# A fused chunk-attention and mixing kernel: x and u turned by DMA transposes, and a new order with the loads in it

## The chip, the cores and the metric

The kernel runs on one core of one Trainium2 chip. The metric is the device time of one execution in microseconds (us). A run is called slow when it is over 1.5% above the fastest run of the same kernel in the same set, and fast otherwise. Means and ratios below use fast runs alone; medians are over all runs. Engines: PE (matmuls), DVE and ACT (vector and scalar work), POOL (issues all loads), SP (SyncE, issues stores and, in the change, transposes).

## The reference

All inputs are float32 in memory; the kernel works in fp16. There are 8 batches, 8 heads, 576 positions, head size 64, model width 512.

```python
# attention in 9 chunks of 64, each for itself
scores = scale * q_c @ k_c.T ;  attn = softmax(scores) ;  x = attn @ v_c    # x: [8, 576, 512]
# mixing
theta = x @ w_theta
zr, zi = x * cos(theta), x * sin(theta)
y  = w_tok_r @ zr + w_tok_i @ zi          # over the 576 positions
u  = x + y
out = u + relu(u @ w_ch)
```

## The kernel before

Two batches make a pair (4 pairs, 1152 rows, 9 tiles of 128 rows); each pair has five groups of one or two tiles, 20 in all. The program is a list of items, searched offline, that fixes the order on every engine. `a1` transposes q and k on PE, `a2` does scores and exp, `a3` attention times V, giving x; `a4` transposes x on PE; `a5` does theta with cos and sin; `z` the products; `tw` transposes the token weights; `yh` and `y` mix over positions and add x, giving u transposed; `w` multiplies u by w_ch; `st` adds and stores. The first number of an item is the pair (in `y`, pair, batch of the pair, block of 128 channels; in `w` and `st`, pair and tile).

```python
ORDER = """
a1.0.0:0 a2.0.0:0 a1.0.1:3 a1.0.2:2 a3.0.0.0:0 a2.0.1:0 a3.0.0.1:0 a2.0.2:0 a3.0.2.0:0
a4.0.0:1 a4.0.2:3 a3.0.1.0:0 a3.0.1.1:0 a5.0.2:0 a4.0.1:1 a5.0.0:0 z.0.2.0:0 z.0.0.0:0
...                                                                      # cut
a2.0.4:0 yh.1.1:0 a3.0.4.0:0 a1.1.0:0 a4.0.3:0 w.0.0:0 a2.1.0:0 a3.0.4.1:0 st.0.0:0
...                                                                      # cut
""".split()

def a4(p, g, bits):                      # x of one group, turned on PE
    ...
    for jj in range(n):
        for db in range(NDB):            # 4 blocks of 128 channels
            nc.tensor.transpose(psv[:, db, jj * P : jj * P + P],
                                st[p]["x", g][:, jj, db * P : db * P + P], id16)
    copy(bits & 1, xT[:, :, x_col(j0) : x_col(j0) + n * P], psv)

def w(p, j):                             # u @ w_ch, and u itself turned back by the identity
    for db in range(NDB):
        nc.tensor.matmul(ps[:, 0:DM], uT[:, db, j * P : j * P + P], wch16[:, db, :], ...)
        nc.tensor.matmul(ps[:, DM + db * P : DM + db * P + P], uT[:, db, j * P : j * P + P], id16)
    nc.scalar.activation(out=r, in_=ps[:, 0:DM], func=AF.Relu)

def out_tile(p, j):
    nc.vector.tensor_tensor(out=o, in0=ps[:, DM : 2 * DM], in1=r, op=ALU.add)
    nc.sync.dma_start(out[...], o)

# loads: in a fixed sequence on POOL; group i is loaded once a1 of group i-7 stands in the program
```

The softmax here doesn't subtract the row's maximum and nothing guards it: scores larger than these inputs give would overflow.

## Time and profile before

| | before |
|---|---|
| time | 219.24 us median of 3 (218.29 to 221.8) |
| span of the profiled run | 217.4 us |
| PE work, by spacings | 190.1 us |
| PE end | 213.1 us, so 23.0 us of PE time lost and a tail of 4.3 us |

### The profile page before, as it was taken

To read this page: it belongs to the slowest core of one execution; us is meant where nothing else is said; L and a number is where in the kernel's file an instruction comes from. 1 tells how busy PE (TensorE), PEld (TensorE's weight loads), DVE (VectorE), ACT (ScalarE), POOL (GpSimd) and SP (SyncE) were. 2 spreads that over 40 slices of the span, in tenths; PEclk is the share of its full clock that TensorE was granted. 3 is DMA by queue.
4 is the path that set the end of the run, shared out by engine and by line. 5 is a ranking of instruction groups with operands and counts; after the bars stand their busy time and mean duration, and the time that the engine had idled before them with its cause. 6 is when DMAs were issued, how large, how long until landed. Compare 5 with 4: busy or idle time off the path is not lost.

```text
span 217.4 us, 6721 instructions
## 1 busy us (share of the span) xinstructions
PE 198.8 (91%) x2994; PEld 138.8 (64%) x2994; DVE 132.8 (61%) x230; ACT 118.5 (54%) x138; POOL 85.1 (39%) x118
## 2 busy tenths in 40 slices
PE   0485999989999999999997999999999999999992
PEld 0374568765677875667886664776766675777750
DVE  0148486747977575869776837567836655275273
ACT  2244484338968689838574468753085446321242
POOL 7896468679885698765920000000000000000000
PEclk9999999999999999999999999999999999999999
DMA  6999999999999999999990012112121313113136
GB/s 59 177 131 166 200 181 179 177 170 132 166 221 196 165 132 181 213 228 192 142 164 5 3 48 72 51 51 48 53 96 51 121 48 100 48 49 147 48 124 216
DMA packets 83612, 26.92 MB, mean 124 GB/s; under 512 B 76288, under 2 KB 78976, under 8 KB 83584
## 3 DMA queue, kind: packets, MB, share of 16 engines
q0 software_dynamic: 77696, 16.54, 86.0%
q1 hardware_dynamic: 5888, 9.96, 13.5%
q8 instruction: 23, 0.38, 0.7%
q14 instruction: 5, 0.04, 0.0%
HBM read 33.06 MB, written 9.44 MB: 195 GB/s over the span
## 4 chain that ended last, share of the span: by engine, by line
PE 80%; DMA 6%; DVE 4%; POOL 3%; issue 3%; ACT 2%; POOLq 0%
PE ps_y L455 28%; PE ps_theta L377 14%; PE ps_uw L475 13%; PE ps_qkT L266 6%; PE ps_y L434 4%; PE ps_sT L292 4%; DMA wtheta<-in_moe_w_theta_dram 3%; PE ps_uw L482 3%; PE ps_xT L348 3%; PE ps_x L320 3%; DMA qk<-in_k_dram 3%; POOL v L176 2%; PE ps_wT L218 1%; POOL qk L155 1%; DVE o L494 1%
## 5 line engine op out<-in xcount | busy, mean ns | idle before, releaser
L455 PE MATMUL ps_y<-wT,z 128*128 128x288 f16 x448 | 59.8, 286 | 1.2 <-issue 1.2
L455 PEld LDWEIGHTS <-z 128*128 128x128 f16 x448 | 42.2, 98 | 13.8 <-issue 1.5
L176 POOL DMA_DIRECT2D v<-in_v_dram x56 | 42.0, 766 | 17.3 <-DMA qk<-in_k_dram 10.7
L475 PE MATMUL ps_uw<-wch,uT 128*128 128x512 f16 x144 | 42.5, 380 | 0.0
L488 ACT ACTIVATE relu<-ps_uw 128x512 f32<-128x512 f32 x36 | 21.6, 600 | 37.6 <-PE ps_uw L482 37.2
L463 DVE TENSOR_TENSOR uT<-ps_y,xT 128x576 f16<-128x576 f32 x28 | 21.2, 755 | 28.8 <-PE ps_y L455 28.7
L494 DVE TENSOR_TENSOR o<-ps_uw,relu 128x512 f32<-128x512 f32 x36 | 24.5, 686 | 11.7 <-ACT relu L488 11.5
L482 PE MATMUL ps_uw<-id,uT 128*128 128x128 f16 x144 | 31.5, 219 | 0.0
L377 PE MATMUL ps_theta<-wtheta,xT 128*128 128x512 f16 x128 | 30.5, 384 | 0.1
L266 PE MATMUL ps_qkT<-id,qk 128*64 128x128 f16 (+1 forms) x640 | 22.5, 227 | 6.4 <-DMA qk<-in_q_dram 5.7
L387 ACT ACTIVATE cos<-ps_theta,pihalf 128x1024 f16<-128x1024 f32 (+1 forms) x20 | 20.6, 1029 | 12.7 <-PE ps_theta L377 12.4
L334 DVE TENSOR_TENSOR x<-ps_x,recip 128x512 f16<-128x512 f32 x36 | 24.9, 691 | 1.2
L266 PEld LDWEIGHTS <-qk 128*64 128x64 f16 (+1 forms) x640 | 19.1, 118 | 8.8 <-DMA qk<-in_q_dram 5.7
L299 ACT ACTIVATE eT<-ps_sT 128x1024 f16<-128x1024 f32 (+1 forms) x20 | 18.3, 940 | 11.4 <-PE ps_sT L292 11.4
L475 PEld LDWEIGHTS <-uT 128*128 128x128 f16 x144 | 14.1, 98 | 14.7
L197 DVE COPY kT<-ps_qkT 128x1024 f16<-128x1024 f16 (+1 forms) x13 | 15.2, 1169 | 12.5 <-ACT qT L199 12.5
L155 POOL DMA_DIRECT2D qk<-in_k_dram x24 | 19.1, 797 | 5.5 <-DMA qk<-in_q_dram 2.9
L377 PEld LDWEIGHTS <-xT 128*128 128x128 f16 x128 | 12.1, 99 | 13.6 <-issue 0.9
L155 POOL DMA_DIRECT2D qk<-in_q_dram x24 | 19.3, 805 | 2.1 <-POOLq L558 0.8
L391 ACT ACTIVATE sin<-ps_theta 128x1024 f16<-128x1024 f32 (+1 forms) x20 | 18.7, 933 | 0.0
L199 ACT COPY kT<-ps_qkT 128x1024 f16<-128x1024 f16 (+1 forms) x7 | 8.4, 1224 | 14.2 <-DVE qT L197 14.2
L292 PE MATMUL ps_sT<-qT,kT 64*64 64x64 f16 x576 | 12.3, 223 | 3.9 <-ACT kT L199 2.9
(51 smaller groups left out, 212.0 us busy)
## 6 DMA issues: line engine op xcount, KB each, us to landing
out_dram<-o SPq DMA_DIRECT2D x32, 256.0 KB, 2.1
qk<-in_q_dram POOLq DMA_DIRECT2D x16, 256.0 KB, 6.9
qk<-in_k_dram POOLq DMA_DIRECT2D x16, 256.0 KB, 8.2
v<-in_v_dram POOLq DMA_DIRECT2D x40, 64.0 KB, 6.4
v<-in_v_dram POOLq DMA_DIRECT2D x16, 128.0 KB, 6.3
out_dram<-o SPq DMA_DIRECT2D x8, 128.0 KB, 2.9
wnat<-in_moe_w_tok_r_dram POOLq DMA_DIRECT2D x2, 288.0 KB, 8.9
wnat<-in_moe_w_tok_i_dram POOLq DMA_DIRECT2D x2, 288.0 KB, 9.6
```

The lines of the kernel that those rows point to most:

```text
L155: nc.gpsimd.dma_start(t[(pp // 2) : (pp // 2) + m // 2, ti].rearrange("p h t d -> p h (t d)"), src.rearrange("h (p t) d -> p h (t d)", t=2),)
L176: nc.gpsimd.dma_start(v16[pp : pp + m, sl, :, 0:D], v[2 * p + bb, :, s0 : s0 + m, :].rearrange("h s d -> s h d"),)
L266: nc.tensor.transpose(psv[par * D : par * D + D, w, e, tk, 0:rows], t[0:rows, w, 2 * e + par, tk, :], id16[0:rows, 0:rows],)
L292: nc.tensor.matmul(psv[kh * CH : kh * CH + CH, par, i, e, :], kT[par * D : par * D + D, e, c0 : c0 + CH], qT[par * D : par * D + D, e, c0 ...
L334: nc.vector.tensor_tensor(out=xo, in0=px[:, :, :, 0:D], in1=recip.broadcast_to((P, 2, NE, D)), op=ALU.mult,)
L377: nc.tensor.matmul(ps[:, jj * DM : jj * DM + DM], xt[:, db, :], wtheta16[:, db, :], start=(db == 0), stop=(db == NDB - 1),)
L455: nc.tensor.matmul(psv[:, hf, 0:HS], zt[:, db * P : db * P + P], wT[:, kt, hf * HS : hf * HS + HS], start=(kt == 0), stop=(kt == 2 * KT),)
L463: nc.vector.tensor_tensor(out=uT_tile(p)[:, db, sl].rearrange("p (f c) -> p f c", f=2), in0=psv[:, :, 0:HS], in1=xT_tile(p)[:, db, sl].rea ...
L475: nc.tensor.matmul(ps[:, 0:DM], uT[:, db, j * P : j * P + P], wch16[:, db, :], start=(db == 0), stop=(db == NDB - 1),)
L482: nc.tensor.matmul(ps[:, DM + db * P : DM + db * P + P], uT[:, db, j * P : j * P + P], id16,)
L488: nc.scalar.activation(out=r, in_=ps[:, 0:DM], func=AF.Relu)
L494: nc.vector.tensor_tensor(out=o, in0=ps[:, DM : 2 * DM], in1=r, op=ALU.add)
```

## The change

Intent: take transposes off PE. x of 18 of the 20 groups and u of the last five batches go through DMA transposes on SyncE; relu and add of those u tiles become one DVE instruction; some stores move to POOL. The list of items was searched again, now with the loads (`lq`, `lv`, `lt`, `lw`, `lc`) as items in it. Bit 16 of an `a4` item selects the DMA; bit 2 of `st` selects POOL.

```diff
-a1.0.0:0 a2.0.0:0 a1.0.1:3 a1.0.2:2 a3.0.0.0:0 a2.0.1:0 a3.0.0.1:0 a2.0.2:0 a3.0.2.0:0
-a4.0.0:1 a4.0.2:3 a3.0.1.0:0 ...
+lw.0:0 lq.0.0:0 a1.0.0:3 lq.0.2:0 lq.0.1:0 a2.0.0:0 a1.0.2:2 lv.0.2:0 a1.0.1:3 a2.0.2:0
+lq.0.3:0 a2.0.1:0 a3.0.2.0:0 a1.0.3:0 lv.0.1:0 a3.0.1.0:0 lq.0.4:0 ...
 (the rest of the two lists is cut)
+    U_DMA = 3
+    def xt(p, g):
+        if n == 1:
+            nc.sync.dma_start_transpose(xm, x[:, 0, :])
+            return
+        for jj in range(n):
+            nc.sync.dma_start_transpose(xT[:, :, c0 : c0 + P], x[:, jj, :])
     def a4(p, g, bits):
+        if bits & 16:
+            xt(p, g)
+            ...
+            return
+    def ut(p, bb, db):
+        nc.sync.dma_start_transpose(un_tile(p, bb)[:, :, db * P : db * P + P], uT_tile(p)[:, db, cols])
     def w(p, j):
-            nc.tensor.matmul(ps[:, DM + db * P : ...], uT[:, db, j * P : j * P + P], id16)
+            if 2 * p + int(j >= KT) < U_DMA:       # only the first three batches
+                nc.tensor.matmul(ps[:, DM + db * P : ...], uT[:, db, j * P : j * P + P], id16)
     def out_tile(p, j, bits):
+            nc.vector.scalar_tensor_tensor(out=o, in0=ps[:, 0:DM], scalar=0.0, in1=un_tile(...)[...],
+                                           op0=ALU.max, op1=ALU.add)
-            nc.sync.dma_start(out[...], o)
+        eng = nc.gpsimd if bits & 2 else nc.sync
+            eng.dma_start(out[...], o)
 (the rule that placed the loads is gone; the cut parts are the same in kind)
```

## The prediction

> **What bounds the kernel now.** I read the page first (busy shares, slices, queues, chain), then the chain in order of time, then the timeline of POOL, which issues all loads. From the page:
>
> ```profile
> span 217.4 us, 6721 instructions
> PE 198.8 (91%) x2994; PEld 138.8 (64%) x2994; DVE 132.8 (61%) x230; ACT 118.5 (54%) x138; POOL 85.1 (39%) x118
> PE   0485999989999999999997999999999999999992
> DMA  6999999999999999999990012112121313113136
> q0 software_dynamic: 77696, 16.54, 86.0%
> PE 80%; DMA 6%; DVE 4%; POOL 3%; issue 3%; ACT 2%; POOLq 0%
> ```
>
> PE is busy almost everywhere after the first slices and carries 80% of the chain. But the DMA row stands at 9 from slice 2 to slice 21 (about 115 us) while the loads run, and then drops to 0 to 3. So there are two resources: PE for the whole span, and the load stream for the first half.
>
> PE's busy time counts latencies that overlap, so I use spacings. From the chain of waits in order of time (start, duration, what):
>
> ```profile
> 14.16 7.46 DMA wtheta<-in_moe_w_theta_dram
> 21.75 1.87 PE ps_theta L377 x4
> ...
> 74.58 1.01 PE ps_qkT L266 x32
> ...
> 161.05 2.21 PE ps_y L455 x18
> 163.25 1.73 PE ps_theta L377 x8
> ...
> 166.06 0.45 PE ps_xT L348 x8
> 166.51 0.22 PE ps_uw L475
> 166.78 0.22 PE ps_uw L475
> ```
>
> Eight PE transposes of x take 0.45 us, that is 56 ns each. A 512-column matmul takes 1.73/8 = 0.216 us. In the last stage (w), matmuls follow each other every 0.27 us (166.51, 166.78), so the identity matmul between two of them costs 0.27 - 0.216 = about 0.056 us. An output tile of w is 4 x 0.27 = 1.09 us.
>
> Summing the whole list of PE work with such spacings: y 28 x 2.25 = 63.0; y of the first batch in halves 9.2; w 36 x 1.09 = 39.2; theta 16 x 1.73 + 4 x 0.86 = 31.1; q/k transposes 16 x 1.01 + 4 x 0.62 = 18.6; scores 8.8; attention x V 9.2; x transposes 16 x 0.45 + 4 x 0.22 = 8.1; token weights 2.7. Total **190 us** of work.
>
> The last PE matmul starts at 212.9 us in the timeline and ACT's last relu, which waits for it, at 213.15, so PE lacks work for 23 us in all. After that come relu (0.60), the last add (0.69) and the last store: 217.4 - 213.15 = 4.3 us of tail.
>
> Where are the 23 us? Just before the first q/k transpose of pair 2, group 1 (started at 74.5) the list holds 53.8 us of work, so 20.7 us are already lost; only 2.3 us are lost later. The early loss is set by loads: the first theta waits for its weights until 21.75. POOL's timeline shows their pace:
>
> ```profile
> 1.24 1.02 POOL L155 DMA_DIRECT2D qk<-in_q_dram  x1 [0.79 <-POOLq L558]
> ...
> 41.29 0.69 POOL L176 DMA_DIRECT2D v<-in_v_dram  x1 [0.69 <-DMA wch<-in_moe_w_ch_dram]
> ...
> 89.67 0.90 POOL L155 DMA_DIRECT2D qk<-in_q_dram  x1
> ...
> 107.95 2.31 POOL L176 DMA_DIRECT2D v<-in_v_dram  x3
> ```
>
> 112 loads are issued from 1.24 to 107.95 + 2.31 = 110.26, one per **0.973 us**; the issue at 41.29 was held until an earlier load had landed, as are most gaps of POOL in the list of waits (10.7 us of waits on k loads alone). The DMA section gives about 6.5 us from issue to landing. Check: before the transpose at 74.5, 67 loads are in line, 1.24 + 67 x 0.973 + 6.5 = 72.9 us. So the present order is just in time for its loads there.
>
> **What the Trainium skill says.** (1) "Perfetto Trace Analysis", Identifying the Most-Contended Engine: matmul busy share does not measure headroom because matmuls are pipelined. The trace agrees: 198.8 us busy for 190 us of work, and each matmul's record (219 to 380 ns) is longer than its spacing. (2) "TensorE: Matmul & The Clock Gate", Step-by-step: what each phase is for: spacing 216 ns at 512 columns and 55.6 ns at 128. The trace gives 0.216 and 0.056 us. (3) "DMA: Bandwidth & Descriptors", Issuing engines are not separate DMA queues: all queues run on the same 16 DMA engines and interleave. So SyncE's transposes meet POOL's loads. How much this costs no trace here shows directly; POOL issued 16 loads from 63.96 to 79.79 (0.99 us each), nearly without stores beside them, and 15 from 79.79 to 95.63 (1.06 us each), with several 256 KB stores beside them. (4) Same page, Latency and other measured facts: a DMA transpose reached 261 GB/s in one kernel. An estimate from it: 128 KB (128 x 512 fp16) takes 0.5 us of all engines. No run yet has one.
>
> **The change, part by part.**
> - x by DMA, 18 of 20 groups: 15 groups of 8 and 3 of 4 transposes leave PE, 132 x 56 ns = **-7.4 us** of PE. Fifteen PSUM copies (DVE 0.68 or ACT 1.01 us each) and three small ones (0.4 to 0.6) go, some 14 us, off the path.
> - u by DMA for five batches: 23 output tiles x 4 identity matmuls = 92 x 56 ns = **-5.2 us** of PE. 23 relus (0.60 us) leave ACT, -13.8 us, off the path except the last: tail -0.6 us. The new single DVE instruction should cost about the old add, 0.69 us.
> - SyncE gets 33 transposes of x and 20 of u. Between x being ready and its theta the new order has 4.7, 5.3 and 5.5 us of PE work for the first three groups and 6 to 20 us for the others; for u 3.4 us at the very last, 6.6 to 40 elsewhere. A transpose that lands within 5 us is hidden.
> - Loads: same bytes, new order; theta's weights first. The w tiles of pair 0, which filled PE around 54 to 96 us, come later (first w after 53 us of PE work, not after 40). So PE work that needs later loads is pulled forward. The tightest point I find is the attention of pair 2, group 1: 68.2 us of PE work stand before it (19 us q/k and scores, 5 attention, 16 theta, 20 y, 4 w, 3 weights, 1 transposes) and its V load is the 92nd, with one POOL store ahead: 1.24 + 93 x 0.973 + 6.5 = 98.2 us. That makes **30 us** lost by then, against 20.7 now.
>
> Sum: PE work 190 - 12.6 = 177.4; + 30 lost early + 2.3 later = 209.7; + tail 3.7 = 213.4 span. The time is 1.9 us above the span before (219.32 against 217.4): **215.3 us**. Without the load limit, at today's 23 us of loss: 177.4 + 23 + 3.7 + 1.9 = **206.0 us**. The PE saving is sure; 9 us of it may go to the loads.
>
> **Rivals.** (A) *PE stays the bound.* For it: the order was searched with the loads inside, which should keep the stream ahead; ACT and DVE get lighter. Against: the load arithmetic above, which fits the kernel before within 2 us. 205 to 208 us. (B) *Loads become the bound in the first 100 us.* For it: DMA at 9 in every early slice. 214 to 216. (C) *B, and transposes slow the loads as well.* Fifteen x transposes stand ahead of that V load, at 0.5 us of all engines each up to +7 us: 216 to 223. For it: shared engines. Against: 256 KB stores hardly slowed the loads. (D) *Transposes land late (over 6 us) and SyncE, which takes them in order with stores and the small z copies (3.8 us to landing now), holds theta up.* Each late group costs PE its excess; ten groups by 1 us would be +10. Against: long distances after the first groups, when the stream is over.
>
> **How the range follows.** I give A 0.4, B 0.3, C and D together 0.3. The mean of 206.5, 215 and 219 is 212.8; I say **213 us**, with 206 to 221 to hold 8 in 10. Faster by over 2% means under 214.9: all of A, half of B, little of C: 0.57. Slower means over 223.6: 0.07. Within 2%: 0.36.
>
> **What would show it.** Right, if ps_xT falls from 144 to 12 transposes, the identity row of ps_uw from 144 to 52, and PE's work sums to about 177 us. B shows as PE waiting for V or q/k loads between 40 and 100 us and the V load of pair 2, group 1 landing near 98 us; A as PE slices at 9 from slice 6 on. C shows as load landings over 8 us and the load stream ending after 120 us. D shows as theta waiting for xT's DMA. The prediction is wrong low if each transpose takes several us of the DMA engines, and wrong high if the load pace improves with the new order.

## More of the kernel before

The main views stand in the prediction. Three more lines matter later. The first is the granted TensorE clock by slice (9 is full), the second the hardware queue that SyncE feeds (packets, MB, share of the 16 engines' span), the third the group of identity matmuls in `w`, which the change removes in part (busy us, mean ns of one, idle before).

```profile
PEclk9999999999999999999999999999999999999999
q1 hardware_dynamic: 5888, 9.96, 13.5%
L482 PE MATMUL ps_uw<-id,uT 128*128 128x128 f16 x144 | 31.5, 219 | 0.0
```

The clock is full throughout, SyncE's queue is nearly idle, and there are 36 tiles x 4 identity matmuls.

**Lost PE time.** All matmuls are in the traces (2994 before), so the items of the order can be counted off against them. At any moment, lost time is the start of the item then on PE minus the sum of the spacings (those of the prediction) of all PE work ahead of it. I use it for every kernel below, because it separates "less work" from "more time lost". It counts two things alike: PE waiting, and PE working at a halved clock, where a matmul takes longer than its spacing. What the second can be worth is given under the table of experiments.

## The result, and the profile after

The change took 234.38 us median of 4 runs (231.39 to 238.47), the kernel before 220.52 us (218.29 to 221.86, 4 runs). The ratio of fast runs is **1.0589**, 95% interval 1.0479 to 1.0699: slower. A ratio here is the mean time of one kernel's fast runs over that of the other's of the same rounds, so it is not quite the ratio of the medians. Two of the change's four runs were fast (231.39 and 231.9) and two slow (236.85 and 238.47). The profiled run is a fast one, with a span of 229.6 us and a mean granted clock of 0.939.

From the page of the changed kernel:

```profile
span 229.6 us, 6323 instructions
PE 191.5 (83%) x2770; PEld 128.1 (56%) x2770; DVE 127.6 (56%) x220; ACT 98.6 (43%) x107; POOL 95.6 (42%) x137
PE   0356775699979397899987999999999999999990
PEclk9998559589999889999997999999999999999999
DMA  4999999999999999999999921793667758437575
q1 hardware_dynamic: 33648, 12.59, 30.7%
PE 35%; DMA 27%; issue 23%; POOL 12%; DVE 2%; POOLq 0%; ACT 0%; SPq 0%
```

PE's busy time fell, but so did its share: slices 2 to 8 stand at 3 to 7 where they stood at 4 to 9, and slice 14 (74.6 to 80.4 us) stands at 3. The DMA row stays at 9 two slices longer. The clock row, flat before, has fives and eights. SyncE's queue moved 33,648 packets in place of 5,888. PE carries 35% of the chain in place of 80%.

What PE waited for, by group (us in total, times, longest), before and then after:

```profile
PE ps_qkT L266 <- DMA qk<-in_q_dram: 5.7, 1, 5.7
PE ps_sT L292 <- ACT kT L199: 2.9, 2, 2.1
```

```profile
PE ps_qkT L277 <- DMA qk<-in_q_dram: 9.1, 1, 9.1
PE ps_theta L410 <- DMA xT<-x: 5.2, 3, 2.7
PE ps_sT L303 <- DVE kT L208: 4.5, 2, 2.4
PE ps_x L331 <- DVE uT L475: 4.0, 1, 4.0
```

The first q load now stands behind theta's weights (9.1 us). Theta waits for transposes of x. Scores wait for the copy of k. The last line is a transpose too, as the chain in order of time shows (start, duration, what):

```profile
69.81 7.80 DMA xTm<-x
...
78.04 0.74 DVE uT L475
78.82 0.43 PE ps_x L331 x16
...
117.89 9.28 DMA xT<-x
127.22 1.04 PE ps_theta L410 x4
```

One 128 KB transpose took 7.80 us. DVE copied what it brought, then did an addition (L475), and PE waited for that addition. The other took 9.28 us, ahead of a theta. The DMA section gives the median from issue to landing:

```profile
xT<-x SPq DMA_TRANSPOSE x30, 6.8
un<-uT SPq DMA_TRANSPOSE x20, 2.7
```

The u transposes, the first of which is issued at 146 us when one V load is left, land in 2.7 us. The x transposes take 6.8 by median: the 19 issued up to 118 us, beside the load stream, landed in 5.7 to 10.2 us, the 14 from 132 us on in 2.4 to 5.1. Two stretches of 20 us, before and then after (stretch, then its length, then busy us and instruction count of PE, PE weight loads, DVE, ACT and POOL, then clock, DMA share, GB/s):

```profile
20.00:40.00 20.00, 18.80 (x267) 12.90 (x268) 12.87 (x25) 11.35 (x12) 13.07 (x17) 1.00 1.65 186
60.00:80.00 20.00, 20.00 (x445) 15.56 (x444) 13.84 (x24) 14.85 (x16) 14.86 (x21) 1.00 1.78 179
```

```profile
20.00:40.00 20.00, 14.23 (x342) 10.29 (x341) 11.91 (x27) 11.26 (x11) 13.41 (x20) 0.66 1.68 160
60.00:80.00 20.00, 14.48 (x382) 11.14 (x381) 10.27 (x18) 9.14 (x9) 13.55 (x18) 0.97 1.94 142
```

PE's busy time fell from 18.80 to 14.23 us in the first, at a mean clock of 0.66, and from 20.00 to 14.48 us in the second, at a clock of 0.97, where waits explain nearly all of it. Loads fall behind as well. The 80th load is issued at 88.6 us (before 78.2), the 90th at 103.3 (86.9), the 110th at 147.9 (108.0). Two things lie beside this. In three stretches of 10 us with x transposes (30 to 50 and 70 to 80 us) the loads' queue moved 3,164 to 3,639 packets, in four without or nearly without (10 to 30 and 50 to 70 us) 8,040 to 8,382; but the count is no measure by itself, since packets differ in size: 110 to 120 us, with four transposes, has 7,768, and the kernel before has 3,968 in 20 to 30 us with none. And POOL stood still ahead of its stores.

```profile
102.74 0.59 POOL L554 DMA_DIRECT2D out_dram<-o  x1 [5.08 <-DVE o L542]
...
143.50 0.57 POOL L554 DMA_DIRECT2D out_dram<-o  x1 [23.07 <-DVE o L542]
```

A store on POOL waits for its data, and the loads queued behind it wait with it: 5.08 us once, and 23.07 us ahead of the last V load. The later delays come mostly with the new order and not with the transposes: in e1 below, which has none, the 80th load is issued at 76.2 us, but the 90th at 99.3 and the 110th at 147.5.

| us | before | after |
|---|---|---|
| PE work | 190.1 | 177.4 |
| lost at 40 / 60 / 80 / 100 us | 18.6 / 20.2 / 20.7 / 22.0 | 26.7 / 31.9 / 38.0 / 42.2 |
| lost at PE's end | 23.0 | 46.8 |
| tail after PE's end | 4.3 | 5.4 |
| span | 217.4 | 229.6 |

So 12.7 us of work went, and 23.8 us of lost time came, together with 1.1 us of tail.

### The profile page after: what moved, and what is told of

Its sections match the earlier page's. It is cut to its first block, busy times and chain, and to the rows that moved or that the text cites. A ratio compares the mean times of both kernels' runs of the same rounds, so it can differ in the third digit from the quotient of the medians.

```text
span 229.6 us, 6323 instructions
## 1 busy us (share of the span) xinstructions
PE 191.5 (83%) x2770; PEld 128.1 (56%) x2770; DVE 127.6 (56%) x220; ACT 98.6 (43%) x107; POOL 95.6 (42%) x137
## 3 DMA queue, kind: packets, MB, share of 16 engines
q1 hardware_dynamic: 33648, 12.59, 30.7%
## 4 chain that ended last, share of the span: by engine, by line
PE 35%; DMA 27%; issue 23%; POOL 12%; DVE 2%; POOLq 0%; ACT 0%; SPq 0%
PE ps_y L488 15%; PE ps_theta L410 7%; DMA v<-in_v_dram 7%; DMA qk<-in_k_dram 6%; DMA qk<-in_q_dram 6%; PE ps_uw L519 5%; POOL qk L165 4%; DMA xT<-x 4%; DMA xTm<-x 3%; POOL out_dram L554 3%; PE ps_qkT L277 3%; POOL v L186 3%; PE ps_sT L303 2%; PE ps_x L331 2%; PE ps_uw L527 1%
## 5 line engine op out<-in xcount | busy, mean ns | idle before, releaser
L554 POOL DMA_DIRECT2D out_dram<-o x19 | 10.4, 551 | 99.0 <-DVE o L542 52.2
L186 POOL DMA_DIRECT2D v<-in_v_dram x56 | 41.9, 769 | 21.6 <-DMA qk<-in_k_dram 7.0
L488 PEld LDWEIGHTS <-z 128*128 128x128 f16 x448 | 42.9, 98 | 14.0
L519 PE MATMUL ps_uw<-wch,uT 128*128 128x512 f16 x144 | 39.0, 386 | 0.0
L410 PE MATMUL ps_theta<-wtheta,xT 128*128 128x512 f16 x128 | 34.0, 409 | 5.3 <-DMA xT<-x 5.2
L277 PE MATMUL ps_qkT<-id,qk 128*64 128x128 f16 (+1 forms) x640 | 24.1, 236 | 12.5 <-DMA qk<-in_q_dram 9.1
L208 DVE COPY kT<-ps_qkT 128x1024 f16<-128x1024 f16 (+1 forms) x13 | 15.2, 1166 | 25.5 <-ACT qT L210 25.5
L277 PEld LDWEIGHTS <-qk 128*64 128x64 f16 (+1 forms) x640 | 20.7, 124 | 14.2 <-DMA qk<-in_q_dram 9.1
L310 ACT ACTIVATE eT<-ps_sT 128x1024 f16<-128x1024 f32 (+1 forms) x20 | 18.5, 938 | 13.6 <-PE ps_sT L303 13.5
L165 POOL DMA_DIRECT2D qk<-in_k_dram x24 | 19.1, 801 | 4.9 <-DMA qk<-in_k_dram 1.5
L165 POOL DMA_DIRECT2D qk<-in_q_dram x24 | 19.2, 807 | 3.6 <-DMA qk<-in_k_dram 1.6
L303 PE MATMUL ps_sT<-qT,kT 64*64 64x64 f16 x576 | 12.8, 223 | 9.4 <-DVE kT L208 4.5
L210 ACT COPY qT<-ps_qkT 128x1024 f16<-128x1024 f16 (+1 forms) x11 | 9.9, 896 | 21.5 <-PE ps_qkT L277 21.5
L424 ACT ACTIVATE sin<-ps_theta 128x1024 f16<-128x1024 f32 (+1 forms) x20 | 18.6, 930 | 0.0
L544 DVE SCALAR_TENSOR_TENSOR o<-ps_uw,un 128x512 f32<-128x512 f32 x23 | 15.6, 688 | 4.9 <-PE ps_uw L519 2.3
L303 PEld LDWEIGHTS <-kT 64*64 64x64 f16 x576 | 9.7, 111 | 11.6 <-DVE kT L208 4.9
```

The lines of the kernel that those rows point to most:

```text
L165: nc.gpsimd.dma_start(t[(pp // 2) : (pp // 2) + m // 2, ti].rearrange("p h t d -> p h (t d)"), src.rearrange("h (p t) d -> p h (t d)", t=2),)
L186: nc.gpsimd.dma_start(v16[pp : pp + m, sl, :, 0:D], v[2 * p + bb, :, s0 : s0 + m, :].rearrange("h s d -> s h d"),)
L277: nc.tensor.transpose(psv[par * D : par * D + D, w, e, tk, 0:rows], t[0:rows, w, 2 * e + par, tk, :], id16[0:rows, 0:rows],)
L303: nc.tensor.matmul(psv[kh * CH : kh * CH + CH, par, i, e, :], kT[par * D : par * D + D, e, c0 : c0 + CH], qT[par * D : par * D + D, e, c0 ...
L310: nc.scalar.activation(out=eT[:, 0:n].rearrange("p i e r c -> p r (i e) c"), in_=psv[:, :, 0:n].rearrange("p r i e c -> p r (i e) c"), fun ...
L410: nc.tensor.matmul(ps[:, jj * DM : jj * DM + DM], xt[:, db, :], wtheta16[:, db, :], start=(db == 0), stop=(db == NDB - 1),)
```

## The experiments

All kernels gave correct results. "New order" and "old order" are the two lists; every kernel but e16, which is the kernel before with a new list, is built from the changed program, which with the old list, the old loads and no transposes builds the same instruction stream as before. "Fast" is the mean of fast runs, of how many of how many; "excess" is that minus the mean of the fast runs of the kernel before of the same call. Lost times come from each profiled run. Ratios marked * are my own quotients of fast means, without an interval, where too few fast runs were there.

| kernel | fast us | excess | ratio (95%) | clock | PE work | lost at 40 / 80 us / end |
|---|---|---|---|---|---|---|
| before | 218.8 to 220.1 | 0 | 1 | 0.998 | 190.1 | 18.6 / 20.7 / 23.0 |
| change | 231.64 (2 of 4) | +12.9 | 1.0589 (1.0479–1.0699) | 0.939 | 177.4 | 26.7 / 38.0 / 46.8 |
| e1_all_on_pe | 237.35 (2 of 4) | +18.0 | 1.082* | 0.957 | 190.1 | 26.2 / 31.2 / 41.4 |
| e2_u_only | 230.26 (3 of 4) | +10.9 | 1.0493 (1.0422–1.0565) | 0.982 | 184.8 | 26.4 / 31.1 / 38.7 |
| e3_x_only | 241.23 (3 of 4) | +21.9 | 1.0993 (1.0901–1.1085) | 0.936 | 182.7 | 24.0 / 37.0 / 50.9 |
| e8_transposes_only | 246.20 (1 of 4) | +27.5 | 1.125* | 0.925, slow | 177.4 | 25.5 / 37.4 / 66.9 |
| e4_shadow_transpose | 235.38 (4 of 4) | +16.0 | 1.0727 (1.0657–1.0797) | 0.965 | 190.1 | 19.2 / 27.5 / 37.3 |
| e5_shadow_pieces | 226.29 (2 of 4) | +6.2 | 1.0272 (1.0143–1.0401) | 0.991 | 190.1 | 19.1 / 24.1 / 28.4 |
| e6_shadow_copy | 224.03 (4 of 4) | +3.9 | 1.0164 (1.0055–1.0272) | 0.997 | 190.1 | 19.3 / 24.5 / 27.7 |
| e7_change_old_loads | 235.84 (3 of 4) | +15.7 | 1.0706 (1.0592–1.082) | 0.982 | 177.4 | 31.2 / 39.5 / 51.6 |
| e9_change_theta_later | 233.99 (3 of 4) | +15.2 | 1.0701 (1.0556–1.0845) | 0.946 | 177.4 | 25.3 / 36.6 / 49.5 |
| e11_change_warm | 237.22 (2 of 4) | +18.5 | 1.084* | 0.961 | 177.4 | 29.0 / 35.4 / 53.8 |
| e14_change_stores_sp | 242.82 (2 of 4) | +23.2 | 1.1051 (1.0992–1.111) | 0.934, slow | 177.4 | 25.3 / 37.3 / 60.7 |
| e12_old_head_x_on_pe | 232.25 (3 of 4) | +12.6 | 1.057 (1.0515–1.0625) | 0.951 | 184.8 | 20.3 / 32.0 / 40.1 |
| e13_old_head_change | 238.83 (4 of 4) | +19.2 | 1.0869 (1.0822–1.0917) | 0.943 | 177.8 | 18.4 / 37.6 / 50.8 |
| e15_head_w_early | 232.91 (4 of 4) | +13.2 | 1.0602 (1.0521–1.0683) | 0.963 | 184.8 | 17.2 / 30.3 / 39.3 |
| e16_before_w_late | 221.71 (4 of 4) | +2.5 | 1.0114 (1.0029–1.0198) | 0.996 | 190.1 | 17.4 / 22.4 / 23.9 |
| l1_late_u | 217.90 (4 of 4) | -2.2 | 0.9891 (0.9811–0.9971) | 0.995 | 185.9 | 17.2 / 19.5 / 23.8 |
| l2_late_u_x | 217.26 (6 of 6) | -1.5 | 0.9935 (0.9843–1.0028) | 0.991 | 184.1 | 17.5 / 20.3 / 28.3 |
| l4_late_u_no_last | 221.27 (5 of 6) | +1.6 | 1.008 (1.0036–1.0124) | 0.99 | 185.9 | 19.4 / 21.6 / 28.4 |

The profiles of e8 and e14 fell in slow runs, so their lost times are shown but not relied on; their fast times are. For e15 and e16 the excess is worked out from the ratio. e11's lost time contains its own 11.3 us of filler matmuls. e8's time is its one fast run; the other three took 250 to 252 us.

**Half clock inside lost time.** Where the clock stood at half, matmuls came at about twice their spacing (theta in the changed kernel 426 ns for 216, x transposes in e1 107 for 56). The extra time is at most the sum of the spacings of the matmuls that started there: 12.6 us in the change, 8.3 in e1, 2.9 in e2, 12.5 in e3, 7.0 in e4, 1.8 in e5, 3.2 in e7, and none before and in e6. The waits proper are then at least 34.2 us in the change, 33.1 in e1, 30.3 in e4, 26.6 in e5, 27.7 in e6 and 48.4 in e7, against 23.0 before. The halved stretches follow stretches of low PE activity (see the point on the clock below), so this part may go back to waits as well; but a difference of lost time isn't one of waits alone.

### Which half costs: the order or the transposes?

The theory: the transposes slow the loads, and the order by itself is harmless. The rival: the new order loses PE time by itself. A variant of each half decides.

**e1_all_on_pe**: the change with every transpose back on PE.

```diff
-... a4.0.0:17 ... a4.0.3:16 ... ut.1.1.1:0 ...        U_DMA = 3
+... a4.0.0:1  ... a4.0.3:0  ... (no ut items) ...     U_DMA = 8
```

> The changed kernel's order and load placement, but x and u turned on PE again: no DMA transpose at all. PE work is 190 us as before. Theory T (DMA transposes in flight take the DMA engines from the loads, so PE waits, and with PE idle its clock is halved as well): the load stream runs at the old pace of about 0.97 us a load and PE lacks work for some 28 us (load arithmetic) instead of 47; 190 + 28 + 4.3 + 1.9 = about 224 us, granted clock 0.97 or more. Rival L (the new order and load placement are bad by themselves): lost PE time stays near 45 us, so 238 us or more.

Measured: +18.0 us, with 41.4 us lost at PE's end. What PE waited for (us in total, times, longest):

```profile
PE ps_xT L381 <- DVE x L341: 4.8, 6, 1.2
PE ps_sT L299 <- DVE kT L204: 4.5, 2, 2.4
PE ps_sT L299 <- ACT kT L206: 3.3, 2, 1.7
```

No DMA transpose flies here, and the order still loses 18.4 us more than the old one; x, turned on PE, and the scores wait for evictions by DVE and ACT. The list brings the new places of the loads and 18 stores on POOL with it; e7 and e14 below look at these. So the rival holds, though not alone, as the next kernels show.

**e2_u_only**: x on PE, u by DMA.

```diff
-... a4.0.0:17 ... a4.0.3:16 ...
+... a4.0.0:1  ... a4.0.3:0  ...      (all a4 items lose bit 16; ut items stay, U_DMA = 3)
```

> The changed order, x turned on PE, u of five batches by DMA as in the change. PE work 185 us. Theory T: the transposes of u start when most loads are done, so nothing is lost to them: about 5 us under the run with all on PE, some 219 us, granted clock as there. Rival L: about 233 us. Rival W (PE waits for late transposes, wherever they are): no gain over the run with all on PE, 224 us or more.

**e3_x_only**: x by DMA, u on PE.

```diff
-    U_DMA = 3
+    U_DMA = 8                        # and no ut items
```

> The changed order, x of 18 groups by DMA as in the change, u on PE. PE work 182.6 us. Theory T: all of the harm is here; lost PE time about 47 us as in the changed kernel, 182.6 + 47 + 4.3 + 1.9 = 236 us, clock near 0.94. Rival L: the same, so this run alone does not tell T from L, but together with the run with all on PE it does. If the harm came from u, this run would be under 225 us.

Against e1, u by DMA saves 7.1 us (18.0 to 10.9; in the profiled runs 5.3 of work and 2.7 of lost time go). x by DMA costs 3.9 us (18.0 to 21.9): it takes 7.4 us of work away and adds 9.5 us of lost time. On top of u it costs 2.0 us (10.9 to 12.9), which the intervals of the two ratios do not separate; e13 against e12 below does (6.6 us). So the x half of the change doesn't pay, even in the order made for it.

**e8_transposes_only**: the old order and the old load sequence with all transposes of the change. By the author's account a first build of it deadlocked before it went to a chip, because u's transposes stood on SyncE ahead of stores that had to free their buffer; they were put behind those.

```diff
 (the old list with loads in the old places)
-a4.0.0:1 ... a4.0.3:0 ...
+a4.0.0:17 ... a4.0.3:16 ... ut.1.1.0:0 ...      U_DMA = 3
```

> The order and loads of the kernel before, with the change's transposes alone: x of the same 18 groups and u of the same five batches by DMA. PE work 177 us. If the shadow run is the whole cost of transposes (14 us of lost PE time), lost is 37 us plus waits of theta for late transposes (this order leaves few us between x and theta, so 5 to 15 us): 222 to 232 us. If the transposes are the main harm of the change it is as slow as the changed kernel, 234 us or more; if the new order is the main harm, it is at least 5 us faster than the changed kernel.

This gives two by two, as excess over before:

| | transposes on PE | transposes by DMA |
|---|---|---|
| old order | 0 | +27.5 |
| new order | +18.0 | +12.9 |

Each half alone makes the kernel slower. The new order is made for the transposes: it cuts their damage, but by itself costs 18.0 us, more than the 12.7 us of work that they save. e8 lies in its case of 234 us or more, far above its first forecast of 222 to 232.

### What does a transpose cost beside the loads?

"Shadow" kernels keep the kernel before whole (all transposes on PE) and add DMAs of x that nobody reads, 33 of 128 KB each, in the places of the x transposes. So only the transfers' pressure on everything else is measured.

**e4_shadow_transpose**:

```diff
 (the old list; behind each of the 18 a4 items a sh item)
+    def sh(p, g):
+        x = st[p]["x", g]
+        for jj in range(GROUPS[g][1]):
+            t = shp.tile([P, NDB, P], FP16, name="shadow")       # 4 buffers
+            nc.sync.dma_start_transpose(t, x[:, jj, :])
```

> The kernel before, unchanged in work and order, plus the 33 DMA transposes of x of the change, written to a scratch tile that nothing reads: PE waits for none of them. Theory T: loads slow down all the same (over 1 us a load while they fly, last load issued after 120 us instead of 110), lost PE time rises from 23 to over 30 us, time 226 us or more. Rival W (the cost is theta waiting for the transposed x): no change, 219 to 221 us.

**e5_shadow_pieces**, the same bytes as ordinary copies in pieces of 256 bytes, the size of nearly all packets of the transposes:

```diff
+            t = shp.tile([P, NDB, 2 * P], FP16, name="shadow")
+            nc.sync.dma_start(t[:, :, 0:P], x[:, jj, :].rearrange("p (a b) -> p a b", b=P))
```

> The kernel before plus 33 plain DMA copies of the same x tiles at the same places, cut into 512 pieces of 256 bytes each like the records of the transposes (about 28,000 more packets on the hardware queue), to a scratch tile that nothing reads. If packets of that size are what slows the loads (theory P), it costs as the shadow transposes did: 231 us or more, lost PE time over 30 us. If it is the transposition in the DMA engines (theory X), near 221 us, lost PE time 23 to 26 us.

**e6_shadow_copy**, the same bytes as ordinary copies of whole rows of 1 KB:

```diff
+            t = shp.tile([P, DM], FP16, name="shadow")
+            nc.sync.dma_start(t, x[:, jj, :])
```

> The same with whole rows of 1 KB, 128 packets a copy. Both theories: 219 to 223 us, lost PE time 23 to 26 us. If it costs over 228 us, neither holds: then any traffic of SyncE beside the loads, or holding the x buffers longer, is what costs.

The DMA sections (count, KB, median us to landing; for a transpose no KB) of e4, then of e6, and e4's waits of PE:

```profile
qk<-in_k_dram POOLq DMA_DIRECT2D x16, 256.0 KB, 9.6
shadow<-x SPq DMA_TRANSPOSE x33, 7.1
```

```profile
shadow<-x SPq DMA_DIRECT2D x33, 128.0 KB, 5.4
qk<-in_k_dram POOLq DMA_DIRECT2D x16, 256.0 KB, 8.8
```

```profile
PE ps_qkT L274 <- DMA qk<-in_q_dram: 7.8, 4, 5.8
PE ps_qkT L274 <- DMA qk<-in_k_dram: 6.1, 6, 2.5
```

Lost PE time at the end is 23.0 us without shadows, 27.7 with whole rows, 28.4 with pieces and 37.3 with transposes. So moving the bytes costs 4.7 us, cutting them small 0.7 more, which the intervals don't separate from nothing, and turning them about **9 us** more. e4 met its theory T; e6 lies just above its forecast, e5 midway between its two. (e5 and e4 had nearly the same number of packets on SyncE's queue, 23,312 and 23,840; that is 17,424 and 17,952 more than before, not the 28,000 of the recorded text.)

Of the 9 us up to 5.2 can be half clock (7.0 us of work in e4, 1.8 in e5), so at least 3.7 are waits. SyncE also needs longer to issue a transpose (1.26 us by median against 0.64 for pieces), and no run separates that from the turning itself. Of the 20 issued before the loads had landed, transposes landed in 7.9 us by median, pieces in 6.6, rows in 6.2; of the 13 later ones in 2.5, 2.3 and 2.1.

The path is visible: k loads land in 9.6 us (8.2 before), the 70th load is issued at 77.3 us (before 69.2), the 100th at 115.1 (99.1), and the first transposes of a group wait for q or k ten times. e8, where theta needs these transposes and u's 20 come on top, loses far more (+27.5 us against +16.0, with 12.7 us less work): the waits of theta for xT there are 22.2 us, in a slow run.

### What in the new order loses PE time?

Four things were altered one at a time in the change; then the head of the list was put back.

**e7_change_old_loads**: the old load sequence in the new order.

```diff
-lw.0:0 lq.0.0:0 a1.0.0:3 lq.0.2:0 ...     (load items as searched)
+lq.0.0:0 lq.0.1:0 lq.0.2:0 lv.0.0:0 ...   (the old sequence, seven groups ahead)
```

> The changed kernel, x and u by DMA as in the change, but with the loads in the old sequence (three groups of q, k and v, then theta's weights, the token weights, the rest, seven groups ahead). Theory O (the new place of the loads costs PE 8 to 14 us in the first 100 us): lost PE time falls from 47 to 35 or so, time about 222 us. If the loads' place is harmless, 231 to 236 us as the changed kernel.

It is no faster (+15.7 us), although its loads are issued about as early as before (the 110th at 109.4 us, before 108.0, change 147.9). Its profiled run has a clock of 0.982 and only 3.2 us of PE work at half clock, and yet the longer span: 235.0 us.

**e9_change_theta_later**: theta's weights behind the first three groups' q and k loads.

```diff
-lw.0:0 lq.0.0:0 a1.0.0:3 lq.0.2:0 lq.0.1:0 a2.0.0:0 ...
+lq.0.0:0 a1.0.0:3 lq.0.2:0 lq.0.1:0 lw.0:0 a2.0.0:0 ...
```

> The changed kernel with one load moved: theta's weights after the first three groups of q and k instead of ahead of all. If the late first q (first PE work at 9.1 us instead of 5.7) is carried to the end, 3 us less than the changed kernel: 231 us. If the early stretch is held by later loads anyway, no change.

PE starts at 5.9 us in place of 9.1, and nothing is left of that at the end: +15.2 us.

**e14_change_stores_sp**: all stores back on SyncE, so that POOL never waits for a store.

```diff
-st.0.1:2 ... st.3.8:2
+st.0.1:0 ... st.3.8:0
```

> The changed kernel with all stores on SyncE again. In the changed kernel POOL waited 5 us for the add ahead of a store at 98 to 103 us, with loads behind it. If this delays needed loads, 3 to 5 us less: 230 us. If the stores on SyncE then hold up transposes behind them, 236 us or more. Else no change.

It is 10 us worse (+23.2): in its profile, a slow one, DVE's adds wait 8.6 us for u transposes (0.8 in the change) and theta 8.7 us for x (5.2), which fits stores holding up the transposes behind them on SyncE. So this run doesn't show by itself that POOL's pauses were harmless. The change does: its first store on POOL comes at 102.7 us, and of its 46.8 us only 4.6 are lost after 95.1.

**e11_change_warm**: dummy matmuls in pair 0, to keep the clock up.

```diff
     def a1(p, g, bits):
+        if p == 0:
+            for _ in range(16):
+                nc.tensor.transpose(ps[:, 0:P], id16, id16)
 (10 and 8 more in a2 and a3)
```

> The changed kernel with dummy matmuls on the identity ahead of each q/k transpose group, score group and attention group of pair 0 (11 us in all), in PSUM that the real ones then overwrite; most fall where PE waits anyway. If PE's halved clock (27 us of the span at half) is a cause of its own, the granted clock rises from 0.94 to 0.97 or more and the time falls by 2 to 6 us. If the clock only follows and costs nothing, the time stays or rises by some us, with the clock up.

The clock rose from 0.939 to 0.961 and the excess from 12.9 to 18.5 us. The 202 fillers at 56 ns are 11.3 us themselves, so this says that filling does not pay, not that the clock is harmless. The clock stayed under the 0.97 at which the test was to tell.

**e12_old_head_x_on_pe** and **e13_old_head_change**: the compute items of the old list up to the first batch's `yh.1.1`, then the remaining items in the new order, with the old load sequence; u by DMA. In e12 x is on PE, in e13 17 groups of x go by DMA (not the 15 of the recorded text).

```diff
-lw.0:0 lq.0.0:0 a1.0.0:3 ... (new order from the start)
+(old items up to yh.1.1) a4.0.3:0 a3.0.4.0:0 ... (then the new order's remaining items)
```

> The change with x on PE and u by DMA (230.8 us, PE loses 38.7 us), but with the old order up to the first batch's y and the old load sequence; the rest in the change's order. If the new head is what loses PE time (theory H), lost is back to 18.6 us at 40 us and about 30 in all: 222 us. If the later order loses it, no gain: 229 us or more.

> The same old head and old load sequence, x of the other 15 groups by DMA as in the change. With theory H 8 us less than the changed kernel, 226 us; the transposes' slowing of the loads remains. If the transposes alone decide, 232 us or more.

The head is repaired: lost time at 40 us is 20.3 and 18.4 us. Then it comes back, 32.0 and 37.6 us at 80 us. So the loss in the first 40 us isn't what costs at the end; the new order's next stretch loses it in any case. e13 against e12 shows the cost of x by DMA once more: +6.6 us (12.6 to 19.2).

**e15_head_w_early** and **e16_before_w_late**: the last suspect. The new order has the first `w` tile of pair 0 at 95.1 us, the old one at 46.4, so that transposes, scores and attention of pair 1 stand bunched, with less other work between them. e15 is e12 with four `w` tiles and their stores moved forward (one store changes from POOL to SyncE); e16 is the kernel before with the same four moved back.

```diff
 e15:  -a1.1.0:2 ... a2.1.0:0 ... a2.1.1:0 ... a4.1.4:1 w.0.0:0 ... w.0.1:0 ... w.0.2:0 ... w.0.3:0
       +a1.1.0:2 w.0.0:0 ... a1.1.2:3 w.0.1:0 ... a1.1.1:0 w.0.2:0 ... a2.1.1:0 w.0.3:0 ... a4.1.4:1
 e16:  -... a4.0.3:0 w.0.0:0 a2.1.0:0 ... w.0.1:0 ... w.0.2:0 ... w.0.3:0 ...
       +... a3.1.4.1:0 w.0.0:0 w.0.1:0 w.0.2:0 w.0.3:0 a1.2.2:3 ...
```

> Old head, old load sequence, x on PE, u by DMA (as the earlier run with the old head), but the four first w tiles of pair 0 are moved forward between the transposes, scores and attention of pair 1, where the kernel before has them. Theory (bunched attention with nothing else for PE to do is what the new order loses after 40 us): lost PE time at 80 us falls from 32.0 to 26 or less and the time from 232.9 to 229 or less; the waits for kT, eT and x in PE's list shrink by some 4 us. Rival (the loss has another cause, such as the clock or the loads): lost at 80 us stays above 30 and the time within 2 us of 232.9.

> The kernel before with only the four first w tiles of pair 0 moved back, from between the transposes and scores of pair 1 to after the attention of pair 1 (as the change has them); no DMA transpose, same loads. Theory: attention of pair 1 then stands bunched and PE loses 3 to 6 us more before 80 us (lost at 80 us 24 to 27 against 20.7), time 222 to 226. Rival: the loads already set the pace there and PE waits for something else anyway; lost at 80 us stays within 1.5 us of 20.7 and the time within 1% of before.

e15: lost time at 80 us goes from 32.0 to 30.3 only, and the time does not move (232.9 against 232.3 us): the rival's case. e16: lost time at 80 us goes from 20.7 to 22.4, just past the rival's 1.5 us and below the theory's 3; the ratio 1.0114 lies below the theory's range of time. So the place of these tiles is worth 1 to 2 us, not 18.

What is left is spread thin. In e1, beyond 60 us, lost time goes from 29.3 to 41.4 us in steps of which the largest is 1.7 us, each at another item. Which property of the list makes these steps isn't settled. That bunched items wait for each other's evictions fits the waits of e1, but e15 and e16 moved only one cause of bunching; the clock falls there as well. This stays open.

### Does it pay where no loads run?

**l1_late_u**: the old order and loads, x on PE, u by DMA for the last four batches, whose transposes are issued after the load stream has ended.

```diff
 (the old list)
-... y.2.0.0:0 ... y.2.0.1:0 a4.3.1:0 ...
+... y.2.0.0:0 ... y.2.0.1:0 ut.2.0.0:0 ... ut.2.0.1:0 ...      U_DMA = 4
```

> The kernel before, its order and its loads, with u by DMA for the four batches of pairs 2 and 3 alone, whose transposes are issued after about 120 us, when the loads are done. PE work falls by 72 x 56 ns = 4.0 us and relu leaves ACT in the tail. If transposes harm only beside the loads (T): lost PE time stays at 23 us, 219.5 - 4.0 - 0.6 = about 215 us. If transposes harm anywhere (landing late, holding up stores): 219 us or more.

Measured: 0.9891 of before, interval below 1. From its page and DMA section (count, median us to landing):

```profile
PE 194.2 (90%) x2922; PEld 134.2 (62%) x2922; DVE 132.2 (61%) x230; ACT 108.1 (50%) x120; POOL 85.1 (39%) x118
un<-uT SPq DMA_TRANSPOSE x16, 2.6
```

The time lies between its two forecasts (215, and 219 or more). The 16 transposes land in 2.6 us. PE has 72 matmuls less, 4.2 us of work (190.1 to 185.9), and the lost time grows by 0.8 us. The tail is 5.7 us in place of 4.3. Of 4.2 us, 2.2 reach the time.

**l2_late_u_x**: batches 3 to 6 in place of 4 to 7, and x of four groups of pair 3 by DMA, straight behind their attention.

```diff
-    U_DMA = 3
+    U_DMA = (3, 4, 5, 6)                  # and the tests become "not in U_DMA"
-a3.3.1.1:0 ... a4.3.1:0 ...
+a3.3.1.1:0 a4.3.1:16 ...                  # in the same way 0, 3 and 4
```

> The order and loads of the kernel before, with DMA transposes only where the loads are over: u of batches 3 to 6 (the last batch stays on PE, so the tail does not wait for a transpose) and x of the four full groups of pair 3, each issued as soon as its x is ready. PE work falls by 18 x 0.22 + 4 x 0.45 = 5.8 us. If lost PE time stays at 23 us and the tail at 4.3 us: 219.5 - 5.8 = 213 to 214 us, under the run with late u alone (217.9). If late x makes theta wait, 216 us or more.

**l4_late_u_no_last**: l2 with x left on PE.

```diff
-a3.3.1.1:0 a4.3.1:16 ...
+a3.3.1.1:0 ... a4.3.1:0 ...
```

> The kernel before with u of batches 3 to 6 by DMA, x all on PE, the last batch's u on PE. PE work 190.1 - 18 x 0.224 = 186 us, tail as before (4.3 us instead of the 5.7 us of the run with late u). With lost PE time at 23 us: 215.3 us. If the transposes that fall beside the last loads (from about 108 us) cost, 217 us or more.

l2 has the lowest mean of all (217.26 us), but that is above the 213 to 214 expected, its interval (0.9843 to 1.0028) includes 1, and it doesn't stand apart from l1. l4 was meant to keep u's gain without l1's longer tail and missed: 1.008. In l4 `w.2.2` waited 3.0 us and in l2 2.1 us for a PSUM buffer, in l1 not. The trace of l4 shows the path. Batches 3 and 5 share one buffer for the turned u, so batch 5's first two transposes on SyncE were issued only at 164.08 us, when the last add of batch 3 was done (163.37 to 164.06). Three stores and the last transpose of batch 4 stood behind them; that one was issued at 169.72, landed at 172.52, and the add that frees the PSUM buffer began at 172.69. In l1 batch 3 is on PE, the same three transposes were issued at 154.12, 156.94 and 164.47 us, and PE did not wait there. No run takes this cause away to measure it.

## Why the prediction was wrong, point by point

The prediction said 213 us, range 206 to 221, with its most likely case faster. Fast runs took 231.64 us.

| term of its sum, us | predicted | measured |
|---|---|---|
| PE work | 177.4 | 177.4 |
| lost before attention of pair 2, group 1 | 30 | 42.3 |
| lost later | 2.3 | 4.5 |
| tail | 3.7 | 5.4 |
| span | 213.4 | 229.6 |

- **PE work: right.** The transposes of x fell from 144 to 12, the identity row of `ps_uw` from 144 to 52, as it said would show.
- **"The attention of pair 2, group 1 ... its V load is the 92nd": the wrong place.** That attention started at 110.6 us with 42.3 us lost, but 42.2 had been lost by 95.1 us, when the first `w` began, and none came from this load: it landed at 109.2 us, 11 later than forecast, and still in time. The prediction read the limit of the early part off one load of a steady stream. In fact there were many small waits from the first item on: 26.7 us at 40 us, 38.0 at 80. This is the failed step, the term "30 lost early": it held that a late load is what makes PE wait, and that the order costs nothing else. What the runs show in its place is the new order itself, 41.4 us lost without a DMA transpose (e1), and in the change still 51.6 with the loads issued about as early as before (e7). By which property of the list stays open.
- **"First w after 53 us of PE work, not after 40": misread.** In the trace of the kernel before the first `w` starts at 46.4 us, after 27.5 us of work, and four are done by 61 us. The new order moved these tiles further than the prediction saw; e15 and e16 put that at 1 to 2 us. Its range for the matmul records, 219 to 380 ns, isn't that of all groups either (192 to 440); nothing rests on it.
- **Rival B, loads as the bound, was right that waiting rises, and wrong in its cause and its size.** It had 23 go to 32.3 us in all. e1 alone, without one DMA transpose, has 41.4, and putting the old load sequence back (e7) gains nothing. What the order lost was not the loads' place.
- **Rival A, "PE stays the bound", 0.4: wrong.** "The order was searched with the loads inside, which should keep the stream ahead" trusted the search. The new order with all work on PE is 18.0 us slower than the old one.
- **Rivals C and D, transposes slow the loads and land late: right in kind, and too cheap.** C gave up to +7 us for 0.5 us of all engines per transpose. In e4 the transposes cost 14.3 us of lost time with nobody waiting for them, 9 us more than copies of the same bytes in pieces. C's other sign, a load stream that ends after 120 us, came (150 us), but it comes in e1 too (149.9). D's landing over 6 us was the median (6.8), with up to 10.2. The prediction gave C and D together 0.3; the change shows the effects of C and D together, on top of what the order loses.
- **"Against: 256 KB stores hardly slowed the loads": no measure for transposes.** Plain copies of the same bytes as the transposes do cost little (4.7 us); the transposes don't behave like them.
- **The tail: 5.4, not 3.7 us.** The relu left the tail as said, and yet it grew; in l1, where only u is by DMA, it grew too, to 5.7.
- **Missing altogether: the clock.** It stood at half in 27 us of the changed kernel: 20.7 to 34.4, 41.2 to 48.0, 78.7 to 82.1 and 123.1 to 126.5 us. The work of 12.6 us done there bounds its direct cost from above. The Trainium skill, "TensorE: Matmul & The Clock Gate", HAM oscillation — how this bites in real kernels, tells that a wait of PE longer than its activity window (about 3.4 us) throttles it, and that what follows then runs at half rate. The trace agrees: the halved stretches are 3.4 us long or multiples of it (13.7, 6.8, 3.4, 3.4), theta comes at 426 ns in place of 216 there, and in the 3.4 us ahead of each PE was busy for 1.34, 1.04, 0.00 and 0.95 us (only one of the four was idle throughout; see the last section). So a wait can cost a second time, in the work after it. How much of the 23.8 us the clock caused and how much it merely followed isn't separated: e7 is slow at a clock of 0.982, e11 slower at 0.961 than the change at 0.939.

Of the 23.8 us of lost time, then: the order brings 18.4 by itself (e1), the DMA transposes in it another 5.4. In the old order they bring far more (e8, +27.5 us). Up to 12.6 of the 23.8 us, and up to 8.3 of the 18.4, can be work at half clock. In no case do the 12.7 us of work saved make up for it.

## What to carry to other kernels

An engine that is busy 91% of the time still only gains from less work if nothing new makes it wait: count work and lost time separately, and try each half of a change (here the order without the transposes) before believing the whole. A DMA transpose is a cheap replacement for matmuls after the load stream has ended (2.6 us to landing, 1% gained in l1), and a dear one beside it (6.8 us by median, and in e4 PE lost 14.3 us with nobody waiting for them). A searched order is no evidence by itself; run it against the old one with everything else equal.

## What the Trainium skill lacked or had wrong

- "Advanced Engine Details and Errata", X-Bar Transpose (TRN2), says that transpose DMAs are as fast as regular ones. Beside a load stream of small packets they aren't: 128 KB landed in 7.1 us by median (e4) against 5.4 (e6) for a plain copy, and 33 of them cost PE 14.3 us of lost time against 4.7. Once the loads were over it holds more nearly: 2.5 us against 2.1.
- "DMA: Bandwidth & Descriptors", DMA Transpose (X-bar), gives constraints but no time, and no page has the time to landing of a 128 x 512 transpose, alone or beside other traffic. Here SyncE needed 1.19 to 3.05 us to issue one of x (median 1.32), and it landed in 5.7 to 10.2 us beside loads and in 2.4 to 5.1 without.
- "TensorE: Matmul & The Clock Gate", What's actually happening, names an idle window of about 3.4 us as what throttles. Here the clock also halved after 3.4 us in which PE had been busy in part. In e1 (stretch, its length, busy us and count of PE, PE weight loads, DVE, ACT, POOL, then clock, DMA share, GB/s):

```profile
86.80:90.20 3.40, 2.04 (x70) 1.41 (x64) 3.27 (x7) 1.56 (x2) 3.40 (x6) 1.00 0.85 54
90.20:93.60 3.40, 3.40 (x16) 1.96 (x17) 1.29 (x2) 1.04 (x2) 0.71 (x2) 0.50 1.20 103
```

  PE was busy for 2.04 of 3.40 us, and then ran at 0.50. In the changed kernel the stretches ahead of the halvings at 20.7 and 41.2 us had PE busy for 1.34 and 1.04 us.
